# DeltaNet and a GELU layer on one core: the order of the head, from the elimination's last turn to the loads of w_out

## The chip, the cores and the metric

The kernel runs on one core of a Trainium2 chip. The metric is the device time of one execution in microseconds (us). Engines: PE (TensorE, matrix products), DVE (VectorE), ACT (ScalarE), POOL (GpSimd), SP (SyncE, which here only issues DMAs). PE's clock is throttled by the chip; the profile shows the clock that was granted, as a share of full speed.

## The reference

```
k_n = k / (norm(k) + 1e-6)
for t in range(S):                                  # B=4, H=8, S=768, D=48
    y[t]   = q[t] @ state                           # state: D x D for each batch and head
    state += beta[t] * outer(k_n[t], v[t] - k_n[t] @ state)
x   = y, reordered to 3072 x 384
h   = x @ w_in                                      # 384 x 2048
out = gelu_exact(h) @ w_out                         # 2048 x 384
```

All is float32. The weights arrive as pairs of 32-bit words, the halves of float64 values, and the kernel makes float32 of them itself.

## The kernel before, in words

**Tiles.** The 768 steps of the recurrence are cut into 12 chunks of 64; within a chunk the recurrence is solved with matrix products. A tile (c, a) is chunk c of two of the four batches: 16 heads, 8 on each half of the 128 partitions. Two chunks form a group g with four tiles, the units u of a = 0 and 1 for either chunk; `Zf`, `Nu` and `XM` hold 32 units of a group.

**The head** (from `by_hand` to `by_hand.close()`) is written out by hand: each of the five engines takes its instructions in the order of the program text. It holds

- turns of K and Q of the first chunks on PE (`transposed`, L419), each copied from PSUM by ACT (L420) into `Kt`, `Qt` or `SQ`; their Gram products (`grams`, `queries`, both through L440), copied by ACT (L451 and its neighbours);
- the elimination of group 0 (`eliminate_steps(0)`): a turn on DVE, then 30 row steps on DVE (L528 and L530), which invert the 32x32 blocks of 32 units at once in `Nu`; then three stream transposes of 128x1024, `back` 0 (L539, to `XM`) and `back` 1 and 2 (L543, to the right and the left half of `Zf`); then `clear` (L560: zeros in the lower left quarter of `Zf`, three memsets on POOL and a multiplication on ACT);
- the joins of the 32x32 blocks to 64x64 (`join`, products `psJ` at L578). Level 0 ends in DVE (L589, from PSUM to `XM`), level 1 in copies to the upper right of `Zf`;
- `against_state` for chunk 0 (V times `ng` on POOL, L722), the masking of the query products P on POOL (`masked`, L474), the scaling of V (L402), then `solve` (psU, L792), `read` (psY, L822), `turn` (x, L882) and `update` (L834) of chunk 0;
- the first decoding of w_in. A weight part goes through `begin` (exponent bits, DVE, L252 or L255), `exponents` (ACT), `mantissas` (two DVE instructions, L272 and L274) and `signed` (DVE, L281 and L282, after which the next raw part is fetched). Part n holds 256 columns of w_in for n < 8, so fc1 of f = 2n and 2n+1 needs it; parts 8 and up are pairs of rows of w_out. From part 3 on `exponents` is a pair of ACT instructions.

**The plan.** Behind the head all steps have a time in chunks, `at(first, last, steps)`; `emit` sorts them by it and writes them. DVE and POOL keep that order. PE's and ACT's instructions are placed by a scheduler, but those handed to `keep` (or `together`, `behind`) stay in the order of the program. fc1 of chunk 0 (L915, 3 matmuls into `psH`, one GELU) begins at plan time 1.0. Around 1.06 to 1.16 stand the load of chunk 3's queries, the join of chunk 1's units (`range(NA, 2 * NA)`), and V of chunk 2.

**Queues.** All loads concerned are issued by SP, one after the other, at some 0.6 us each. Before, the six transfers of w_out's first three parts (`fetch(n_in)` to `fetch(n_in + 2)`, into `w_raw`) are issued in the head ahead of V of chunk 1 (`load_v(1)`); the fourth part, which lies in the spare half of `G`, follows in the plan at 1.36.

**Two waits between engines that matter here:** `psH` and the unread products' `psI` take the PSUM tag "mlp" of two buffers, so fc1 of f + 2 waits for the GELU of f; the `sq` and `dn` tags have two buffers each as well.

Of the kernel before, what the change touches and what calls it, by code (L numbers as in the profile page):

```python
# [8 lines left out]
F32 = mybir.dt.float32  # L9
# [5 lines left out]
ALU = mybir.AluOpType  # L15
# [4 lines left out]
def kernel(  # L20
# [28 lines left out]
    nc = tc.nc  # L49
    B, H, S, D = q.shape  # L50
    DM, DF = moe_w_in.shape
    C = 64
    HB = 32
    NC = S // C
    NP = H // 2
    NA = B // 2
# [18 lines left out]
    def sq(name, *shape):  # L75
        return small[0].tile([128, *shape], F32, tag="sq", name=name)
# [189 lines left out]
        else:  # L266
            put(nc.scalar.activation, e, e, ACT.Relu, bias=lim[:, 0:1], scale=float(2 ** 23))

    def mantissas(n):
        dst, lo, hi, e = halves[n]  # L270
        bits = dst.bitcast(U32)
        nc.vector.tensor_scalar(bits, hi, 0xFFFFF, 0x100000, op0=ALU.bitwise_and,  # L272
                                op1=ALU.bitwise_or)
        nc.vector.scalar_tensor_tensor(dst, lo, 2.0 ** -32, bits, ALU.mult, ALU.add)  # L274

    def signed(n):

# [44 lines left out]
    def factors(gm, bt_, n):  # L322

        nc.vector.tensor_scalar_add(n, n, 1e-6)
        r = wk.tile([128, 2 * NA, H], F32, tag="r", name="r", bufs=1)[:, 0:n.shape[1]]
        nc.vector.reciprocal(r, n)
        nc.vector.tensor_tensor(gm, bt_, r, op=ALU.mult)
        nc.vector.tensor_tensor(gm, gm, r, op=ALU.mult)
# [144 lines left out]
    def masked(u, engine=nc.gpsimd):  # L473
        engine.tensor_tensor(u.P, u.P, mask_h, op=ALU.mult)  # L474
# [16 lines left out]
    def eliminate_steps(g):  # L491
        steps = []
        rows_on = nc.gpsimd if g > 1 else nc.vector

        def scales():
            gt = wk.tile([128, HB], F32, tag="gt", name="gt", bufs=1)
            gl = XMs[g] = wk.tile([128, NU, HB], F32, tag="XM", name="XM", bufs=1)
            nc.vector.transpose(gt, gms[g].rearrange("q t h -> q (t h)"))
            wide = gt.unsqueeze(2).to_broadcast([128, HB, HB])
            if g == 0:  # L500
                nc.gpsimd.tensor_tensor(gl, low, wide, op=ALU.mult)
            else:
                nc.gpsimd.affine_select(out=gl, in_=wide, compare_op=ALU.is_ge, fill=0.0, base=-1,
                                        pattern=[[1, HB], [-1, HB]], channel_multiplier=0)

        def flip():
            Nus[g] = wk.tile([128, HB, HB], F32, tag="Nu", name="Nu", bufs=1)
            nc.vector.transpose(Nus[g], Ds[g].rearrange("q u n -> q n u"))
            if g < 2:
                scaled_flip()  # L510

        def scaled_flip():
            rows_on.tensor_tensor(Nus[g], Nus[g], XMs[g], op=ALU.mult)

        def eliminate(j):
            nu = Nus[g]
            n = HB - 1 - j
            if j == 1 or n == 1:
                to = (slice(2, HB), slice(0, 1)) if j == 1 else (slice(HB - 1, HB), slice(0, j))
                by = (slice(2, HB), slice(1, 2)) if j == 1 else (slice(j, j + 1), slice(0, j))  # L520
                factor = nu[:, 1, 0:1] if j == 1 else nu[:, j + 1, j:j + 1]
                if g < 2:
                    nc.vector.scalar_tensor_tensor(nu[:, to[0], to[1]], nu[:, by[0], by[1]], factor,
                                                   nu[:, to[0], to[1]], ALU.mult, ALU.add)
                    return
            tmp = wk.tile([128, HB * HB // 4], F32, tag="tmp", name="tmp", bufs=1)
            tmp = tmp[:, 0:n * j].rearrange("q (i c) -> q i c", i=n)
            rows_on.tensor_tensor(tmp, nu[:, j + 1:, j:j + 1].to_broadcast([128, n, j]),  # L528
                                  nu[:, j:j + 1, 0:j].to_broadcast([128, n, j]), op=ALU.mult)
            rows_on.tensor_tensor(nu[:, j + 1:, 0:j], nu[:, j + 1:, 0:j], tmp, op=ALU.add)  # L530

        def diagonal():
            flat = Nus[g].rearrange("q i c -> q (i c)")
            rows_on.memset(flat[:, 0:HB * HB:HB + 1], 1.0)

        def back(x):
            nu = Nus[g]
            if x == 0:
                nc.vector.transpose(XMs[g].rearrange("q u c -> q c u"),  # L539
                                    nu.rearrange("q i c -> q c i"))  # L540
            elif x == 1 or g == 0:
                cols = slice(HB, C) if x == 1 else slice(0, HB)
                nc.vector.transpose(Zf[g % 2][:, :, cols].rearrange("q u i -> q i u"), nu)  # L543
            else:
                for p in range(2):
                    top = slice(p * C, p * C + HB)
                    if g > 2:
                        nc.gpsimd.tensor_copy(Zf[0][top, :, 0:HB], Zf[0][top, :, HB:C])
                    else:
                        nc.scalar.copy(Zf[0][top, :, 0:HB], Zf[0][top, :, HB:C])  # L550

        def clear(g):
                for cc in range(2):
                    for p in range(2):
                        part = Zf[g % 2][p * C + HB:(p + 1) * C,
                                         cc * NU // 2:(cc + 1) * NU // 2, 0:HB]
                        if g == cc == p == 0:
                            nc.scalar.mul(part, low[0:HB, 0:HB // 2], 0.0)
                        else:
                            nc.gpsimd.memset(part, 0.0)  # L560

        steps = [(0.3, scales), (3.0, flip)] + ([(1.2, scaled_flip)] if g > 1 else [])
        steps += [(0.7, eliminate, j) for j in range(1, HB - 1)]
        steps += [(0.1, diagonal)]
        steps += [(1.9, back, x) for x in range(3)]
        return steps + [(0.0, clear, 0)] if g == 0 else steps

    def join(g, ts, level, copy=nc.scalar.copy):

# [339 lines left out]
    def fc1(c, f):  # L909
        if c == 1 and f < EARLY:  # L910
            psH = dn("psH")[:, 0, 0:NA * 128]
        else:
            psH = ps.tile([128, NA * 128], F32, tag="mlp", name="psH")
        for m in range(NM):
            nc.tensor.matmul(psH, lhsT=w_in_sb[:, f // 2, m, f % 2 * 128:(f % 2 + 1) * 128],  # L915
                             rhs=xTs[c][:, m, :], start=(m == 0), stop=(m == NM - 1))
        gelu = G[:, :, f, :], psH.rearrange("q (a n) -> q a n", a=NA), ACT.Gelu
        if c == 0 or f < EARLY:
            keep(nc.scalar.activation, *gelu)
        else:  # L920
            nc.scalar.activation(*gelu)  # L921

    def send(u, cols=slice(0, DM), queues=None):
        queues = queues or ((nc.sync, nc.sync) if 0 < u.c < NC - 1 else (nc.scalar, nc.scalar))
# [89 lines left out]
    def keep(fn, *args, **kw):  # L1014
        i = fn(*args, **kw)  # L1015
        if free:
            tc.keep_in_program_order(i)
# [201 lines left out]
    signs(0, 2)  # L1219
    diagonals(first[3])  # L1220
    root(n0)
    scales_, flip_, *rows, back0, back1, back2, clear_ = [s_[1:] for s_ in eliminate_steps(0)]
    factors(gms[0], beta_m[:, 0:2].rearrange("q c a h -> q (c a) h"), n0)
    scales_[0]()
    flip_[0]()
    ng = wk.tile([128, NA, H], F32, tag="ng", name="ng", bufs=1)
    for u in first:
        grams([u])
    signs(2, NC)
    third = [tiles[2, a] for a in range(NA)]  # L1230
    sums_ = [(u, h) for u in third for h in range(H)]
    for u in first:
        transposed(u, (1,))
        if u.c == 1:
            for x in sums_[5 * u.a:5 * u.a + 5]:
                sum_of_squares(*x)
        queries([u])
    for a in range(NA):
        fetch_q(tiles[2, a])
# [1 line left out]
        fetch_in(Qp[2 + a][:, :, 0:D], k, tiles[3, a])  # L1241
    for n in range(2, NS):
        fetch(n)
    for n in range(n_in, n_in + 3):
        fetch(n)
    load_v(1)
    for u in third:
        transposed(u, (0,))
    for x in sums_[10:13]:
        sum_of_squares(*x)  # L1250
    grams(third)
    for u in third:
        transposed(u, (1,))
    for x in sums_[13:]:
        sum_of_squares(*x)
    fourth = [tiles[3, a] for a in range(NA)]
    for u in fourth:
        transposed(u, (0,))
    grams(fourth)
    for fn, *args in rows:  # L1260
        fn(*args)
    nc.vector.scalar_tensor_tensor(ng, gms[0][:, 0:NA], -1.0, ns[0], ALU.mult, ALU.mult)
    back0[0](*back0[1:])
    against_state(first[:NA])
    for u in first:
        masked(u)
    back1[0](*back1[1:])
    for a in range(NA):
        join(0, (a,), 0)
    back2[0](*back2[1:])  # L1270
    for a in range(NA):
        join(0, (a,), 1)
    clear_[0](*clear_[1:])
    for u in first[NA:]:
        scale_v(u)
    begin(0)
    exponents(0)
    mantissas(0)
    begin(1)
    mantissas(1)  # L1280
    solve(first[:NA])
# [27 lines left out]
    def state_at(c, *times, first=(), second=(), last=()):  # L1309

        steps = state_steps(c, first, second, last)
        if len(times) > len(steps):
# [5 lines left out]
    plan += [decode_in(), at(1.365, 1.9, decode_steps(n_in, NW)), at(1.91, 1.911, [(1.0, late)])]  # L1318
    rows1, join1 = eliminate_steps(1), join_steps(1)
    plan += [at(1.06, 1.065, [(1.0, load, 3)]),  # L1320
             [(t, (join, 0, range(NA, 2 * NA), level)) for level, t in enumerate((1.085, 1.16))],
]
    sums = [(1.0, sum_of_squares, tiles[3, a], h) for a in range(NA) for h in range(H)]
# [148 lines left out]
```

## Time and profile before

| what | us |
|---|---|
| median of 3 runs | 627.55 (626.76 to 627.88) |
| profiled execution | 626.5 |
| its span (first to last instruction) | 624.7 |
| row steps on DVE | 17.36 to 38.94 |
| the three turns on DVE, with the level 0 joins among them | 39.04 to 46.93 |
| chunk 0's solve to its update on PE | 47.91 to 56.0 |
| first fc1 on PE | 56.01 |
| six transfers of w_out issued by SP | 37.61 to 41.24 |
| first read of w_out's raw words on DVE (part 8) | 80.02 |

A page of the profile gives the busy time of each engine, the span in 40 slices with the granted clock (PEclk), the chain of work that ended last, and groups of instructions. A timeline lists start, length, engine, source line, operation, output<-inputs, shape and, in brackets, the idle time before an instruction and whose end ended it. In the weights' decoding `w_out_sb` stands for raw words of w_in, which are staged in its memory.

POOL's and SP's timelines of the stretch:
```profile
40.69 4.96 POOL L474 TENSOR_TENSOR P<-P,mask 128x512 f32<-128x512 f32 x4
47.21 2.18 POOL L560 MEMSET Zf<- 32x512 f32 x3 [1.55 <-DVE Zf L543]
51.71 2.63 POOL L402 TENSOR_TENSOR V<-V,n 128x384 f32<-128x384 f32 x2 [2.32 <-DMA V<-in_v_dram]
```
```profile
37.61 3.63 SPq L234 DMA_DIRECT2D w_raw<-in_moe_w_out_dram  x6
41.29 4.73 SPq L100 DMA_DIRECT2D V<-in_v_dram  x4
75.61 1.10 SPq L234 DMA_DIRECT2D G<-in_moe_w_out_dram  x2
```

PE's timeline from 31 to 45 us, turns (L419), Grams (L440) and joins (L578):
```profile
35.06 1.62 PE L419 MATMUL psT<-ident,Qp 128*128 128x128 f32 x8
38.21 1.15 PE L419 MATMUL psT<-ident,Qp 128*128 128x128 f32 x8 [1.53 <-ACT SQ L420]
39.98 1.98 PE L440 MATMUL psG<-Kt 48*64 48x64 f32 x64 [0.62 <-ACT Kt L420]
41.90 1.06 PE L578 MATMUL psJ<-XM,G 32*32 32x32 f32 x32
```

### The profile page before, as it was taken

The page shows a single profiled execution, that of the slowest core. Times are in us where ns is not written, and L with a number is a line of the kernel's source. Part 1 is how long each engine was busy: PE and PEld are TensorE (multiplying, and loading weights), DVE is VectorE, ACT ScalarE, POOL GpSimd, SP SyncE. Part 2 cuts the span into 40 slices and gives each one's busy share as a digit, 9 for nine tenths or more (in the row PEclk, how much of TensorE's full clock was granted, in tenths as well). Part 3 has the DMA queues.
Part 4 walks back from the last instruction along what each step waited for, and adds up shares of the span by engine and source line. Part 5 has one row for each costly group of instructions (what it writes and reads, how often), then busy time and mean ns, then how long its engine had stood idle before and what let it go on. Part 6 is the DMA issues. An engine that isn't in the chain of part 4 may idle for free.

```text
span 624.7 us, 19703 instructions
## 1 busy us (share of the span) xinstructions
PE 604.7 (97%) x8358; PEld 539.8 (86%) x8358; DVE 440.4 (70%) x811; ACT 240.5 (39%) x546; POOL 212.8 (34%) x316
## 2 busy tenths in 40 slices
PE   6789999999999999999999999999999999999997
PEld 5578786676799999998899998899998899988997
DVE  7999899988967697774859755859745947332532
ACT  3576876265443165224451134451134222044200
POOL 4045002000369821687222885222885200000000
PEclk9976999999999999999999999999999999999999
DMA  9686775101433452353123533013421001010011
GB/s 130 162 269 164 168 185 136 25 1 37 72 41 50 76 92 39 56 115 39 16 44 54 92 73 38 13 31 55 75 50 17 12 3 27 4 24 1 0 27 26
DMA packets 159576, 39.64 MB, mean 63 GB/s; under 512 B 151168, under 2 KB 154368, under 8 KB 159488
## 3 DMA queue, kind: packets, MB, share of 16 engines
q1 hardware_dynamic: 156816, 37.34, 30.7%
q10 hardware_dynamic: 2672, 1.03, 0.8%
q8 instruction: 66, 1.08, 0.7%
q14 instruction: 22, 0.18, 0.1%
HBM read 33.62 MB, written 4.72 MB: 61 GB/s over the span
## 4 chain that ended last, share of the span: by engine, by line
PE 88%; DVE 5%; ACT 3%; DMA 2%; issue 1%; SPq 0%; ACTq 0%
PE psX L966 13%; PE psY L1032 11%; PE psY L966 9%; PE psX L1032 8%; PE psZ L1032 6%; PE psV L1032 6%; PE psH L915 5%; PE psO L933 4%; PE psZ L966 4%; PE psV L966 4%; PE psG L440 3%; PE psK L732 3%; PE psY L822 2%; PE psU L792 2%; PE psQ L752 2%; PE psT L419 2%
## 5 line engine op out<-in xcount | busy, mean ns | idle before, releaser
L377 POOL TENSOR_TENSOR n<-n,half 128x16 f32<-128x16 f32 x10 | 30.8, 3079 | 178.8 <-DVE n L375 131.0
L530 POOL TENSOR_TENSOR Nu<-Nu,tmp 128x30 f32<-128x30 f32 (+14 forms) x120 | 65.3, 544 | 9.4
L528 POOL TENSOR_TENSOR tmp<-Nu 128x30 f32<-128x30 f32 (+14 forms) x120 | 62.5, 520 | 9.4
L1032 PE MATMUL psX<-xT,w_in_sb 128*128 128x256 f32 (+1 forms) x288 | 62.6, 346 | 0.0
L966 PE MATMUL psX<-w_out_sb,G 128*128 128x192 f32 x320 | 56.1, 329 | 0.0
L966 PEld LDWEIGHTS psX<-w_out_sb,G 128*128 128x128 f32 x320 | 52.2, 190 | 0.7
L1032 PEld LDWEIGHTS psX<-xT,w_in_sb 128*128 128x128 f32 x288 | 47.9, 190 | 5.4
L915 PE MATMUL psH<-xT,w_in_sb 128*128 128x256 f32 x192 | 44.6, 386 | 2.3 <-ACT G L921 1.1
L915 PEld LDWEIGHTS psH<-xT,w_in_sb 128*128 128x128 f32 x192 | 36.0, 191 | 9.6 <-ACT G L1015 2.5
L933 PE MATMUL psO<-w_out_sb,G 128*128 128x384 f32 x128 | 43.9, 490 | 0.0
L851 DVE TENSOR_TENSOR V<-psY,y 64x192 f32<-64x192 f32 (+1 forms) x60 | 21.3, 356 | 30.4 <-PE psY L834 26.4
L1060 DVE TENSOR_TENSOR psY<-psY,pu 128x512 f32<-128x512 f32 x20 | 14.0, 700 | 40.3 <-PE psY L1032 40.3
L1032 PE MATMUL psY<-xT,w_in_sb 128*128 128x256 f32 (+1 forms) x192 | 41.5, 345 | 0.0
L1015 ACT COPY xT<-psX 128x768 f32<-128x768 f32 x9 | 7.2, 800 | 79.8 <-PE psX L892 79.8
L1015 ACT COPY pu<-psZ 128x512 f32<-128x512 f32 x40 | 23.5, 587 | 37.5 <-PE psZ L1032 35.0
L933 PEld LDWEIGHTS psO<-w_out_sb,G 128*128 128x128 f32 x128 | 23.5, 190 | 14.2 <-issue 0.3
L1032 PEld LDWEIGHTS psY<-xT,w_in_sb 128*128 128x128 f32 x192 | 32.1, 191 | 3.5
L1015 ACT ACTIVATE G<-G 128x512 f32<-128x512 f32 x40 | 25.2, 631 | 21.2 <-DVE G L1068 21.0
L1068 DVE TENSOR_TENSOR G<-psY,pu 128x512 f32<-128x512 f32 x20 | 13.8, 690 | 22.2 <-PE psY L1032 21.5
L1015 ACT ACTIVATE G<-psY 128x512 f32<-128x512 f32 x20 | 11.9, 596 | 45.2 <-PE psY L1032 45.2
L966 PE MATMUL psY<-w_out_sb,G 128*128 128x192 f32 x160 | 28.1, 329 | 0.0
L966 PE MATMUL psZ<-T,pu 128*128 128x192 f32 x160 | 28.1, 329 | 0.0
(208 smaller groups left out, 1376.2 us busy)
## 6 DMA issues: line engine op xcount, KB each, us to landing
Kp<-in_k_dram SPq DMA_DIRECT2D x76, 96.0 KB, 3.2
w_out_sb<-in_moe_w_in_dram SPq DMA_DIRECT2D x24, 256.0 KB, 4.4
V<-in_v_dram SPq DMA_DIRECT2D x48, 96.0 KB, 3.1
w_raw<-in_moe_w_out_dram SPq DMA_DIRECT2D x12, 384.0 KB, 4.4
out_dram<-o_sb SPq DMA_DIRECT2D x40, 96.0 KB, 2.2
Qp<-in_k_dram SPq DMA_DIRECT2D x64, 32.0 KB, 2.2
G<-in_moe_w_out_dram SPq DMA_DIRECT2D x4, 384.0 KB, 5.1
Qp<-in_q_dram SPq DMA_DIRECT2D x96, 16.0 KB, 2.0
```

Source lines behind the costliest of these rows:

```text
L377: nc.gpsimd.tensor_tensor(flat, flat, half, op=ALU.pow)
L440: nc.tensor.matmul(psG[HALF[p], r, i * NP + j, :], lhsT=u.Kt[rows, p, j, :], rhs=(u.Qt if x else u.Kt)[rows, p, j, :], start=True, stop=True)
L528: rows_on.tensor_tensor(tmp, nu[:, j + 1:, j:j + 1].to_broadcast([128, n, j]), nu[:, j:j + 1, 0:j].to_broadcast([128, n, j]), op=ALU.mult)
L530: rows_on.tensor_tensor(nu[:, j + 1:, 0:j], nu[:, j + 1:, 0:j], tmp, op=ALU.add)
L732: nc.tensor.matmul(u.psK[HALF[p], r, j, :], lhsT=u.Kt[rows, p, j, :], rhs=SQ[rows, u.a, p ^ r, j, 0:w], start=True, stop=True)
L851: nc.vector.tensor_tensor(dst, src, pairs(u.y[at_], s), op=ALU.add)
L915: nc.tensor.matmul(psH, lhsT=w_in_sb[:, f // 2, m, f % 2 * 128:(f % 2 + 1) * 128], rhs=xTs[c][:, m, :], start=(m == 0), stop=(m == NM - 1))
L933: nc.tensor.matmul(u.psO, lhsT=G[:, u.a, f, :], rhs=w_out_sb[:, f, :], start=(f == 0), stop=(f == NF - 1))
L966: nc.tensor.matmul(ps_, lhsT=lhs[:, f, :], rhs=rhs[:, f, :], start=first and f == 0, stop=f == FH - 1, skip_group_check=not first)
L1015: i = fn(*args, **kw)
L1032: nc.tensor.matmul(ps_[:, i], lhsT=lhs[:, f // 2, f % 2 * 128:(f % 2 + 1) * 128], rhs=rhs, start=first and i == 0, stop=True, skip_group_c ...
L1060: nc.vector.tensor_tensor(L1["Y1"], L1["Y1"], L1["pu"][:, 0], op=ALU.add)
```

## The change

- **Third turn.** `back` 2 of group 0 is gone. The upper left of `Zf` is copied from its upper right by ACT (`upper_left`): units 0 to 15 behind `back` 1 and ahead of the joins, units 16 to 31 at plan time 1.05, kept in order. The lower left is cleared by two memsets on POOL ahead of the elimination. `clear` is gone.
- **Joins.** Level 1 of a = 1 is copied by DVE instead of ACT, between the two instructions of part 0's `mantissas`; `begin(0)` and `exponents(0)` come ahead of level 1.
- **Q.** Each tile of chunks 0 and 1 is turned before the query products of the tile ahead of it; K of chunk 2 likewise.
- **Unread products.** PE multiplies the identity by columns of a K tile into a PSUM tile that nobody reads. A semaphore ties the first of each set to a row step on DVE.
- **Chunk 3's Gram** comes after row step 24; its turns after row step 22. Sums of squares of chunk 2 are spread anew over ACT's list.
- **Loads.** The six w_out transfers go from the head to plan time 1.1.
- **GELUs.** All of fc1's GELUs are handed to `keep`.
- **V times `ng`** of a = 1 goes behind three of the P masks on POOL.

The diff, cut to its core:

```
-        steps += [(1.9, back, x) for x in range(3)]
-        return steps + [(0.0, clear, 0)] if g == 0 else steps
+        return steps + [(1.9, back, x) for x in range(3 if g else 2)]
+
+    def upper_left(us, put=lambda fn, *args: fn(*args)):
+        for p in range(2):
+            top = slice(p * C, p * C + HB)
+            put(nc.scalar.copy, Zf[0][top, us, 0:HB], Zf[0][top, us, HB:C])
...
-        if c == 0 or f < EARLY:
-            keep(nc.scalar.activation, *gelu)
-        else:
-            nc.scalar.activation(*gelu)
+        keep(nc.scalar.activation, *gelu)
...
     factors(gms[0], beta_m[:, 0:2].rearrange("q c a h -> q (c a) h"), n0)
+    for p in range(2):
+        nc.gpsimd.memset(Zf[0][p * C + HB:(p + 1) * C, :, 0:HB], 0.0)
     scales_[0]()
...
+    transposed(first[0], (1,))
+    for u, after in zip(first, first[1:] + [None]):
+        if after:
+            transposed(after, (1,))
+        else:
+            signs(2, NC)
+            transposed(third[0], (0,))
         queries([u])
...
-    for n in range(n_in, n_in + 3):
-        fetch(n)
     load_v(1)
-    for u in third:
-        transposed(u, (0,))
-    for x in sums_[10:13]:
+    transposed(third[1], (0,))
+    for x in sums_[:4]:
         sum_of_squares(*x)
     grams(third)
     for u in third:
         transposed(u, (1,))
-    for x in sums_[13:]:
+    for x in sums_[4:10]:
         sum_of_squares(*x)
-    for u in fourth:
-        transposed(u, (0,))
-    grams(fourth)
...
+    def unread(*cols, after=None):
+        psI = (sq("psI", 512) if after is None else
+               ps.tile([128, 512], F32, tag="mlp", name="psI"))
+        for n in cols:
+            nc.tensor.matmul(psI[:, 0:n], lhsT=ident,
+                             rhs=Kp[0].rearrange("q h d -> q (h d)")[:, 0:n], start=True, stop=True)
+            if after is not None:
+                tc.add_manual_dep(latest(mybir.EngineType.PE), after.name, ...)
+                after = None
+
+    between = {**{j: (256, 128) for j in (19, 20, 21)}, **{j: (256,) for j in (22, 23, 24, 26, 27, 28, 29, 30)}}
     for fn, *args in rows:
         fn(*args)
+        if args and args[0] in between:
+            unread(*between[args[0]], after=latest(mybir.EngineType.DVE))
+        if args and args[0] == 22:
+            for u in fourth:
+                transposed(u, (0,))
+        if args and args[0] == 24:
+            grams(fourth)
+            for x in sums_[10:]:
+                sum_of_squares(*x)
     nc.vector.scalar_tensor_tensor(ng, gms[0][:, 0:NA], -1.0, ns[0], ALU.mult, ALU.mult)
+    unread(256, 256, 256, 256, 128, after=latest(mybir.EngineType.DVE))
     back0[0](*back0[1:])
-    against_state(first[:NA])
-    for u in first:
+    against_state(first[:1])
+    for u in first[:3]:
         masked(u)
+    against_state(first[1:NA])
+    masked(first[3])
     back1[0](*back1[1:])
+    upper_left(slice(0, NA * H))
     for a in range(NA):
         join(0, (a,), 0)
-    back2[0](*back2[1:])
-    for a in range(NA):
-        join(0, (a,), 1)
-    clear_[0](*clear_[1:])
+    unread(256, 256, 128)
+    begin(0)
+    join(0, (0,), 1)
+    exponents(0)
+    mantissas(0, (0,))
+    join(0, (1,), 1, nc.vector.tensor_copy)
+    mantissas(0, (1,))
     for u in first[NA:]:
         scale_v(u)
-    begin(0)
-    exponents(0)
-    mantissas(0)
...
+             at(1.05, 1.051, [(1.0, upper_left, slice(NA * H, NU), keep)]),
+             at(1.1, 1.102, [(1.0, fetch, n_in + i) for i in range(3)]),
```

More of the change, by code (lines that the diff above doesn't have):

```diff
@@ L267, in exponents, with mantissas @@
             put(nc.scalar.activation, e, e, ACT.Relu, bias=lim[:, 0:1], scale=float(2 ** 23))
-    def mantissas(n):
+    def mantissas(n, part=(0, 1)):
         dst, lo, hi, e = halves[n]
         bits = dst.bitcast(U32)
-        nc.vector.tensor_scalar(bits, hi, 0xFFFFF, 0x100000, op0=ALU.bitwise_and,
-                                op1=ALU.bitwise_or)
-        nc.vector.scalar_tensor_tensor(dst, lo, 2.0 ** -32, bits, ALU.mult, ALU.add)
+        if 0 in part:
+            nc.vector.tensor_scalar(bits, hi, 0xFFFFF, 0x100000, op0=ALU.bitwise_and,
+                                    op1=ALU.bitwise_or)
+        if 1 in part:
+            nc.vector.scalar_tensor_tensor(dst, lo, 2.0 ** -32, bits, ALU.mult, ALU.add)
     def signed(n):
@@ L540, in back @@
                                     nu.rearrange("q i c -> q c i"))
-            elif x == 1 or g == 0:
-                cols = slice(HB, C) if x == 1 else slice(0, HB)
-                nc.vector.transpose(Zf[g % 2][:, :, cols].rearrange("q u i -> q i u"), nu)
+            elif x == 1:
+                nc.vector.transpose(Zf[g % 2][:, :, HB:C].rearrange("q u i -> q i u"), nu)
             else:
@@ L550, in back @@
                         nc.scalar.copy(Zf[0][top, :, 0:HB], Zf[0][top, :, HB:C])
[L552 to L558, printed above, removed]
-                        else:
-                            nc.gpsimd.memset(part, 0.0)
         steps = [(0.3, scales), (3.0, flip)] + ([(1.2, scaled_flip)] if g > 1 else [])
@@ L917, in fc1 @@
         gelu = G[:, :, f, :], psH.rearrange("q (a n) -> q a n", a=NA), ACT.Gelu
-        if c == 0 or f < EARLY:
-            keep(nc.scalar.activation, *gelu)
-        else:
-            nc.scalar.activation(*gelu)
+        keep(nc.scalar.activation, *gelu)
     def send(u, cols=slice(0, DM), queues=None):
@@ L1221 @@
     root(n0)
-    scales_, flip_, *rows, back0, back1, back2, clear_ = [s_[1:] for s_ in eliminate_steps(0)]
+    scales_, flip_, *rows, back0, back1 = [s_[1:] for s_ in eliminate_steps(0)]
     factors(gms[0], beta_m[:, 0:2].rearrange("q c a h -> q (c a) h"), n0)
+    for p in range(2):
+        nc.gpsimd.memset(Zf[0][p * C + HB:(p + 1) * C, :, 0:HB], 0.0)
     scales_[0]()
@@ L1228 @@
         grams([u])
-    signs(2, NC)
-    third = [tiles[2, a] for a in range(NA)]
+    third, fourth = [[tiles[c, a] for a in range(NA)] for c in (2, 3)]
     sums_ = [(u, h) for u in third for h in range(H)]
-    for u in first:
[L1233 to L1236, printed above, removed]
+    transposed(first[0], (1,))
[5 more added lines that the diff above has]
+            transposed(third[0], (0,))
         queries([u])
@@ L1253, with latest @@
         transposed(u, (1,))
-    for x in sums_[13:]:
+    for x in sums_[4:10]:
         sum_of_squares(*x)
-    fourth = [tiles[3, a] for a in range(NA)]
-    for u in fourth:
-        transposed(u, (0,))
-    grams(fourth)
+    def latest(engine):
+        return next(i for i in reversed(nc.cur_bb.bb.instructions) if i.engine == engine)
+    def unread(*cols, after=None):
[5 more added lines that the diff above has]
+            if after is not None:
+                tc.add_manual_dep(latest(mybir.EngineType.PE), after.name,
+                                  mybir.DependencyInfo(mybir.DependencyClass.Sync,
+                                                       mybir.DependencyReason.DATA),
+                                  reason="time")
+                after = None
@@ L1262 @@
     nc.vector.scalar_tensor_tensor(ng, gms[0][:, 0:NA], -1.0, ns[0], ALU.mult, ALU.mult)
+    unread(256, 256, 256, 256, 128, after=latest(mybir.EngineType.DVE))
     back0[0](*back0[1:])
-    against_state(first[:NA])
-    for u in first:
+    against_state(first[:1])
+    for u in first[:3]:
         masked(u)
+    against_state(first[1:NA])
+    masked(first[3])
     back1[0](*back1[1:])
+    upper_left(slice(0, NA * H))
     for a in range(NA):
         join(0, (a,), 0)
-    back2[0](*back2[1:])
```

## The prediction

> **What bounds the kernel now.** I read the totals and slices first, then the chain that ended last, then the timelines of DVE, ACT and PE from 38 to 70 us, where every edit lies.
>
> The page's totals and three of its slice rows (40 slices of 15.6 us):
> ```profile
> span 624.7 us, 19703 instructions
> PE 604.7 (97%) x8358; PEld 539.8 (86%) x8358; DVE 440.4 (70%) x811; ACT 240.5 (39%) x546; POOL 212.8 (34%) x316
> ...
> PE   6789999999999999999999999999999999999997
> ...
> DVE  7999899988967697774859755859745947332532
> ...
> PEclk9976999999999999999999999999999999999999
> ```
> PE (TensorE) is at 9 tenths or more from the fourth slice on, and PEclk, the granted clock, is below full in the first four alone. So a change in the head is worth what it moves PE's first dense work, and no more. In windows, PE is busy 5.87 of 6 us from 70 to 76 and all of 76 to 104. In the chain that ended last DVE stands from 44.3 to 66 (the elimination's end, then the decoding of w_in), PE and ACT from 66 to 76, PE to 88, DVE to 103, then PE to the end.
>
> DVE's timeline (start, length, instruction, in brackets its idle time before and who ended it):
> ```profile
> 43.02 0.86 DVE L589 TENSOR_TENSOR XM<-psJ,gm 32x256 f32<-32x256 f32 x2
> 44.27 0.86 DVE L589 TENSOR_TENSOR XM<-psJ,gm 32x256 f32<-32x256 f32 x2 [0.39 <-PE psJ L578]
> 45.16 1.93 DVE L543 STREAM_TRANSPOSE Zf<-Nu 128x1024 f32<-128x1024 f32 x1
> 46.93 0.55 DVE L255 TENSOR_SCALAR w_e<-w_out_sb 128x768 uint32<-128x768 uint32 x1
> 47.39 0.97 DVE L272 TENSOR_SCALAR w_in_sb<-w_out_sb 128x768 uint32<-128x768 uint32 x1
> ...
> 49.74 0.55 DVE L272 TENSOR_SCALAR w_in_sb<-w_out_sb 128x768 uint32<-128x768 uint32 x1
> ```
> DVE hardly rests: whatever leaves its list brings w_in forward. ACT's and PE's timelines where decoding, GELUs and joins meet:
> ```profile
> 61.53 2.12 ACT L1015 ACTIVATE w_e<-w_e,lim 128x768 f32<-128x768 int32 x2 [1.93 <-DVE w_e L252]
> 63.52 0.35 ACT L1015 ACTIVATE G<-psH 128x256 f32<-128x256 f32 x1
> 63.77 2.11 ACT L1015 ACTIVATE w_e<-w_e,lim 128x768 f32<-128x768 int32 x2
> ...
> 67.37 1.17 ACT L593 COPY Zf<-psJ 32x512 f32<-32x512 f32 x2 [1.00 <-PE psJ L578]
> ```
> ```profile
> 61.53 1.56 PE L915 MATMUL psH<-xT,w_in_sb 128*128 128x256 f32 x6
> 63.93 1.56 PE L915 MATMUL psH<-xT,w_in_sb 128*128 128x256 f32 x6 [0.83 <-ACT G L1015]
> ...
> 66.14 1.19 PE L578 MATMUL psJ<-Zf,XM 32*32 32x32 f32 x62 [0.48 <-DVE XM L589]
> ```
> The chain here is: DVE writes the raw exponents of part 3, ACT maps them for 2.12 us, only then comes the GELU of f2, which frees the PSUM tile that fc1 of f4 waits for (0.83 us). After 67.27 PE waits for next to nothing.
>
> **The change part by part.** First DVE, up to part 0's L255.
>
> *Third turn gone.* L589 ends at 45.13, L255 starts at 46.93: −1.80. *psJ in time.* The 0.39 before the second L589 goes if psJ is ready: −0.39. *Two copies from PSUM added* (join level 1 of a=1, 32x256): the nearest row is L589, same shape and source, 0.86 for two: +0.86. *Clearing of Zf.* POOL's memsets (47.21, 2.18 us) lay over L272, 0.97 against 0.55 for the same line at 49.74; they move to the start: −0.42. There, as two ops of 32x1024, they lie around 7 to 10 us, ahead of the scaling of `low` at 14.15; by the same row they can lengthen a DVE op there by 0 to 0.5, and I take 0, since DVE waits in that stretch anyway.
>
> *New neighbours.* POOL masks P from 40.69 to 45.65 in four ops of 1.24. L255 of part 0 now starts while the fourth runs. Nearest row: L255 at 53.69 beside POOL's scaling of V (51.71 to 54.34) took 1.07 against 0.55. Between 0 (L255 comes after 45.65) and the length of a whole mask op, 1.24; I take +0.75, between that and the row's 0.51. The two stretched ops beside the scaling of V (1.47 against 0.96, 1.07 against 0.55) stay.
>
> [...]
>
> *Unread products.* Identity times Kp, 256 columns each, after rows 19 to 30, after `ng` and between the joins. Nearest row: fc1 (L915) has the same width; in the chain x12 take 2.86 and x24 take 5.38 us, 0.21 for one record, and a product is two: 0.43 at the full clock, double at half. After `ng` (38.9) stand 4 of 256 and one of 128: 2.0 us. PE's order before psJ is now: turns of chunk 3, two products, Gram, five products, these, psJ. Chunk 3's K is issued up to 32.6 and lands between 35.0 and 37.3. Landing at 35.5: turns to 36.1, Gram to 37.7, five products to 39.9, `ng` products to 41.9, psJ half a microsecond per half: ready before L589 can start at 43.02. Landing at 37.3: everything 1.6 to 2.2 later, psJ at 44 to 44.6, DVE waits 1.0 to 1.6. These same microseconds clear the collision with P. So from 0 to +1.6 in place of, not beside, the +0.75.
>
> Sum for DVE: −1.80 −0.39 +0.86 −0.42 +0.75 = **−1.0**, with bounds −1.75 (no collision, psJ in time) and +0.24 (−1.80 +0.86 −0.42 +1.6: psJ 1.6 late), more if the products also run slow.
>
> The clock, which the products concern, in the windows view (PE, PEld, DVE, ACT, POOL busy, then granted clock):
> ```profile
> 39.50:39.70 0.20, 0.00 (x0) 0.00 (x0) 0.20 (x1) 0.20 (x1) 0.20 (x1) 0.77 0.83 287
> 39.70:40.00 0.30, 0.02 (x3) 0.02 (x3) 0.30 (x1) 0.30 (x2) 0.30 (x2) 0.50 0.75 287
> 56.00:57.00 1.00, 1.00 (x7) 0.87 (x4) 1.00 (x2) 0.40 (x1) 1.00 (x1) 0.66 0.06 16
> 57.00:57.50 0.50, 0.50 (x4) 0.43 (x3) 0.47 (x2) 0.00 (x0) 0.50 (x1) 1.00 0.06 25
> ```
> PE ran at half clock from 39.6 to about 56.7, through both joins, psU, psY and the turns of x (dense from 47.91 to 56.01). With products in place of the pause 36.7 to 38.2 I expect it fast. That halves some 8 us of PE, but f0 to f3 then wait for w_in's parts, which DVE sets: worth 0 to 0.4 by itself.
>
> *Upper-left copies on ACT.* Two in place of the third turn's first half, 32x512 from SBUF to SBUF; nearest row, the diag copies of the same shape, 1.24 for two. The first pair runs from about 43, while DVE does L589, and psJ level 1 doesn't read it; psU does, which PE reaches later: 0. The second pair is issued behind part 3's exponents and ahead of f2's GELU: **+1.24** on the chain ACT to f4. Thus f4 starts at 63.93 − 1.0 + 1.24 = +0.24 later. *What takes it up:* PE's 0.48 in front of psJ level 1 falls, since its L589 comes 1.0 earlier on DVE. It leaves f5 and all behind it at +0.24 − 0.48 = −0.24; the first 0.7 us of fc1, which ran at half clock from 56.01, are worth 0.3 more: about **−0.5**. In short, the end moves by DVE's shift + 0.46. From there PE is dense, so −0.5 is carried to the end.
>
> *Q turned one tile ahead.* PE waited 0.67 us four times (21.63 to 30.19) for ACT's copies of Q; they go, but the third Gram waits for K and DVE's rows (17.36 to 38.94) wait for none of it: 0. If it failed, the row steps would still set 38.94. *Squares of chunk 2* (20, 0.14 to 0.2 each) move inside ACT's idle time: 0.
>
> *w_out later.* Six transfers of 384 KB leave SP's queue at 37.61 (3.63 us of issuing) and go to 75.6, in front of chunk 4's K (76.76). V of chunk 1 is issued 3.7 earlier and POOL's 2.32 us wait for it goes; what follows at 76.76 comes some 3.6 later, needed from about 100 on. The first of w_out lands, at 6 to 7 us apiece beside each other, at about 79 to 80; DVE's first read of it is at 80.02. A wait of 0 to 1.0: I take 0, since DVE waits 0.53 and 0.35 for PE near 87 and catches up there. *GELUs in order*: their order in ACT's list is unchanged: 0.
>
> Total: −0.5 against the profiled 626.5 (span 624.7 and 1.8 around it), so 626.0. That execution is 1.05 under the median of 627.55; on the median I get **627.0**.
>
> **The rivals.**
> *Better cover.* K lands by 35.5 and L255 misses the P op, or loses 0.4 at most: DVE −1.75, f4 at 63.93 − 1.75 + 1.24 = −0.51, with psJ's 0.48 and the faster f0 make −1.3; if f4's wait on the GELU (0.83) shrinks too, because f2 itself is ready sooner, up to −2.1: **625.8** in the middle. For it: most transfers of these 10 us land 2.4 to 3.0 us after their issue, which is 35 to 35.6. Against: L255 at 44 to 45 falls in front of 45.65 as worked out.
>
> *Products hold up psJ (slower).* The change doesn't do what it says if the clock falls at 39.6 all the same. Then the `ng` products take 3.9 instead of 2.0. With K at 35.5 they end at 43.8, the first psJ half (1.06 at that clock) at 44.8, L589 is 1.8 late and DVE at +0.24; each 0.1 us that K is later costs 0.2. With K at 36.0 DVE is at about +1.2, f4 at +2.4, less 0.48 and with no gain of clock: +2.0 at the end, **629.5**; with K at 37.3 it is up to +5. It eats the whole gain from 0.9 us of psJ's delay on (−1.36 + 0.9 + 0.46), and is slower by 0.2% from 1.9 on. For it: PE has a fixed order and the products stand ahead of psJ; against: the two turns on DVE leave 4 us between the rows' end, 38.94, and 43.02, and the products themselves fill the pause after which the clock fell.
>
> [...]
>
> *w_out comes late.* Landing 2.5 us after DVE's read at 80.02, beyond the slack of 0.9: −0.5 + 1.6, **628.6**.
>
> **How the numbers follow.** Forecast 0.42, of it 0.06 below 626.3; better cover 0.32; held-up psJ 0.15; pause moved 0.07; w_out late 0.04. A measurement of this kernel tells 0.2%, or 1.25 us, from no change. Faster 0.32 + 0.06 = 0.38; slower 0.15 + 0.07 + 0.02 = 0.24, and 0.02 more for an unhidden w_out: 0.26; same 0.36. Range: 624.8 (better cover at its far end, 625.4, with the two ops beside V's scaling also gone, 0.5) to 630.0 (the pause at 3.4 less f4's 0.83 is +2.6).
>
> **What would show it.** Right: no third turn, L255 of part 0 at about 45.9; granted clock 1.00 from 36 to 57; first f4 near 64.2; f5 near 66.8; PE dense behind it. Wrong: psJ level 0 after 43; L255 at 47 or later; clock 0.50 anywhere past 57; part 8's L255 with DVE idle ahead of it; f4's wait on GELU over 1.5.

## The result, and the profile after

| | before | changed |
|---|---|---|
| median, us | 627.62 (4 runs) | 633.02 (4 runs, 631.65 to 633.75) |
| profiled execution, us | 626.5 | 633.3 |
| span, us | 624.7 | 631.6 |

The ratio is 1.0086, 95% interval 1.0066 to 1.0106: 5.4 us slower, where 0.5 faster was forecast and 630.0 was the end of the range. The changed kernel's page (totals, and the granted clock over 40 slices of 15.8 us):

```profile
span 631.6 us, 19804 instructions
PE 609.0 (96%) x8402; PEld 542.3 (86%) x8402; DVE 438.6 (69%) x812; ACT 242.0 (38%) x547; POOL 211.2 (33%) x315
...
PEclk9879899999999999999999999999999999999999
```
PE has 44 records more (22 unread products, two records each) and 4.3 us more busy time; its clock is below full in the fifth slice too.

A good first reading sets the same instruction of both traces beside each other and lists how late the changed kernel is. On DVE:

| before, at | late by | what happened just ahead |
|---|---|---|
| 19.3 | 0.7 | PE waited 0.81 instead of 0.25 near 13, the diagonal blocks came later |
| 44.3 | 2.7 | L589 (now L585) waited for psJ |
| 57.2 | 0.6 | the removed turn and the vanished collisions gave it back |
| 77.2 | 2.6 | f4 waited, then ran at half clock |
| 83.4 | 3.7 | DVE waited for w_raw |
| 91 to 316 | 3.5 | nothing: PE is dense in both |
| 327.2 | 5.5 | PE stood still for 1.90 us |
| 420.0 to the end | 6.8 to 6.9 | PE stood still for 0.96 us |

DVE behind the second turn, in the changed kernel's timeline (start, length, instruction, idle time before):
```profile
46.12 1.75 DVE L585 TENSOR_TENSOR XM<-psJ,gm 32x256 f32<-32x256 f32 x4 [2.33 <-PE psJ L574]
47.90 0.65 DVE L255 TENSOR_SCALAR w_e<-w_out_sb 128x768 uint32<-128x768 uint32 x1
...
49.10 0.86 DVE L589 COPY Zf<-psJ 32x256 f32<-32x256 f32 x2
```
The wait for psJ, 0.39 before, is 2.33, and the two added copies take 0.86 as forecast. PE's timeline says why, and shows the later pause ahead of f4:
```profile
33.23 4.90 PE L1258 MATMUL psI<-Kp,ident 128*128 128x256 f32 x14
...
41.07 4.37 PE L1258 MATMUL psI<-Kp,ident 128*128 128x256 f32 x20
45.38 1.20 PE L574 MATMUL psJ<-XM,G 32*32 32x32 f32 x64
...
65.77 2.92 PE L911 MATMUL psH<-xT,w_in_sb 128*128 128x256 f32 x6 [2.79 <-ACT G L1008]
```
The first 14 records (six of them with 128 columns only) take 0.35 each and the 20 ahead of psJ 0.22. But for turns and a Gram (37.93 to 41.07, two products among them) PE does nothing else from 33.2 on, and psJ stands behind all of it. ACT's timeline around the pause:
```profile
62.09 2.13 ACT L1008 ACTIVATE w_e<-w_e,lim 128x768 f32<-128x768 int32 x2 [2.73 <-DVE w_e L252]
64.09 1.21 ACT L1008 COPY Zf<-Zf 32x512 f32<-32x512 f32 x2
65.33 0.38 ACT L1008 ACTIVATE G<-psH 128x256 f32<-128x256 f32 x1
```
The second pair of copies stands, 1.21 us long, in front of f2's GELU, which frees f4's tile. The windows view (PE, PEld, DVE, ACT, POOL busy, then the granted clock) of the three stretches:
```profile
33.00:37.40 4.40, 4.40 (x16) 3.86 (x15) 3.99 (x13) 2.41 (x14) 0.00 (x0) 0.50 0.90 208
62.90:65.70 2.80, 0.07 (x1) 0.00 (x0) 2.51 (x4) 2.73 (x5) 0.00 (x0) 0.99 0.81 238
65.80:69.20 3.40, 3.40 (x31) 2.39 (x32) 3.30 (x6) 2.64 (x4) 0.00 (x0) 0.52 0.95 278
```
The early products ran at half clock; the pause of 2.8 us is followed by 3.4 us at half clock, in which fc1's six records take 2.92 instead of 1.56. Last, on DVE and on PE, two waits that the head's order doesn't show:
```profile
85.68 0.56 DVE L255 TENSOR_SCALAR w_e<-w_raw 128x768 uint32<-128x768 uint32 x1 [1.00 <-DMA w_raw<-in_moe_w_out_dram]
```
```profile
326.23 0.97 PE L959 MATMUL psZ<-T,pu 128*128 128x192 f32 x5 [1.90 <-issue]
```
"issue" means that PE waited for nothing that the profile shows.

### The profile page after: what moved, and what is told of

The parts are those of the page before. It is cut to its first block, busy times and chain, and to the rows that moved or that the text cites. A ratio compares the mean times of both kernels' runs of the same rounds, so it can differ in the third digit from the quotient of the medians.

```text
span 631.6 us, 19804 instructions
## 1 busy us (share of the span) xinstructions
PE 609.0 (96%) x8402; PEld 542.3 (86%) x8402; DVE 438.6 (69%) x812; ACT 242.0 (38%) x547; POOL 211.2 (33%) x315
## 3 DMA queue, kind: packets, MB, share of 16 engines
q8 instruction: 66, 1.08, 0.7%
## 4 chain that ended last, share of the span: by engine, by line
PE 85%; DVE 4%; DMA 4%; SPq 3%; issue 2%; ACT 2%; ACTq 0%; DVEq 0%
PE psX L959 13%; PE psY L1025 11%; PE psY L959 8%; PE psX L1025 8%; PE psV L1025 6%; PE psZ L1025 6%; PE psO L926 4%; PE psZ L959 4%; PE psV L959 4%; PE psH L911 3%; PE psK L728 3%; PE psY L818 2%; SPq L100 2%; DMA Kp<-in_k_dram 2%; PE psG L442 2%
## 5 line engine op out<-in xcount | busy, mean ns | idle before, releaser
L911 PE MATMUL psH<-xT,w_in_sb 128*128 128x256 f32 x192 | 46.1, 393 | 5.3 <-ACT G L1008 4.6
L911 PEld LDWEIGHTS psH<-xT,w_in_sb 128*128 128x128 f32 x192 | 36.4, 194 | 13.4 <-ACT G L1008 7.0
```

## The experiments

**Theory:** the loss is a sum of parts that have little to do with one another: late w_out, the second pair with the clock that falls behind it, products ahead of psJ, and PE's stalls of 1.90 and 0.96 us. **Rival:** one part makes the others late, so that undoing it brings most of the loss back. The kernel before, run on the same chip beside each group of them, had medians of 627.0 to 627.3. Runs of one kernel with products spread by 2 to 5 us, so differences under about 1 us between such medians are not told apart.

**w_out back.**
```
+    for n in range(n_in, n_in + 3):
+        fetch(n)
     load_v(1)
...
-             at(1.1, 1.102, [(1.0, fetch, n_in + i) for i in range(3)]),
```


> Changed kernel with the six w_out transfers issued in the head again, ahead of V of chunk 1. Theory (the loss is a sum of parts, and late w_out is one of them: DVE waited 1.00 us for w_raw at 84.7 and its lag grew from 2.6 to 3.7 there): 1.0 us faster than the changed kernel's 633.0, so 632.0, with no DVE wait on w_raw. Rival (those waits are covered by DVE's later waits for PE): 633.0 within 0.3. The two stalls of PE without a visible releaser, 1.90 us at 324 and 0.96 at 418, stay if they belong to PE's own instruction stream, which is the same here, and go if they were caused by the loads.

632.63 us (631.08 to 633.06): the wait for w_raw is gone, but the time falls by 0.4 only, which is within the spread. In the trace the pause ahead of f4 is still 2.79 and DVE waits up to 3.3 us for ACT behind it. Undoing one of several parts measures only what the next one leaves. PE's stalls are there (1.66 and 0.68): the w_out loads didn't make them.

**Pair early.**
```
-    upper_left(slice(0, NA * H))
+    upper_left(slice(0, NU))
...
-             at(1.05, 1.051, [(1.0, upper_left, slice(NA * H, NU), keep)]),
```


> Changed kernel with both pairs of upper-left copies in the head, behind the second turn, none in front of f2's GELU. Theory (the second pair, 1.21 us on ACT, lengthens PE's wait ahead of f4 from 0.83 to 2.79, and this pause drops the clock to half from 65.8 to 69.2): f4 waits 1.2 to 1.6, no half clock near 66, f5 2.0 to 2.6 earlier, 630.7. Rival (the pause is set by DVE's part 3 alone and the clock falls anyway): f4 at most 0.6 earlier, 632.4 or more.

632.30 us (630.35 to 633.93). f4's wait is 1.52, and f5 follows at 0.23 us a record, without half clock, as the theory had it, 1.6 earlier (2.0 to 2.6 expected); but DVE now meets w_raw earlier and waits 2.1 for it, and the time moves by 0.7, within the spread, where 2.3 was expected. In the profiled execution, the slowest of the four, the lead over the changed kernel was down to 0.6 at PE's first stall, and there more was lost:
```profile
325.64 4.34 PE L959 MATMUL psZ<-T,pu 128*128 128x192 f32 x16 [1.90 <-issue]
```
The granted clock is 0.50 from 325.5 to 328.8, so these 16 records take 4.34 instead of 2.76, and the kernel ends 0.6 later than the changed one. In this trace half clock thus stands behind the stall; behind the changed kernel's, as long, the granted clock is 1.00 from 324 to 331.

**No products, and no late products.** All of `unread`'s calls out, or those behind `ng` and between the joins.

> Changed kernel without any unread product; all of the reference is still computed. Theory (products at half clock filled PE from 33.2 to 45.4 and held psJ back; DVE waited 2.33 for it): psJ level 0 before 43.0, no wait of DVE there, part 0's L255 2.3 us earlier at about 45.6, f4 earlier by as much: 630.9. Rival (the products keep the clock up; without them psJ, psU and psY run at half clock and eat the gain): clock 0.50 from 40 to 57 and 632.5 or more.

> Changed kernel with the products of the row steps, but without the 4.5 behind ng and the 2.5 between the joins. Theory: the 2.0 us of products right ahead of psJ are the part that delays it; DVE's wait falls from 2.33 to about 0.4, L255 2 us earlier, with the clock still full from 38 on: 631.1, no slower than the kernel without any product. Rival (the delay comes from the products at rows 19 to 24, which ran at half clock): DVE's wait stays above 1.5 and the time near 632.5.

628.07 us (10 runs) without any: the largest step, −5.0, more than the 2.1 expected. psJ is in time, L255 at 44.90. The clock is 0.50 around the joins (64 records of psJ take 1.92 and 1.95, where they took 1.20 in the changed kernel), as the rival has it, and the gain is there all the same. PE's two stalls are gone. Without the late ones 629.2 (631.1 expected): DVE's wait is gone too (L585 at 43.02), so the theory's half about psJ holds, but one stall of 0.78 stays near 415, and f4 waits 2.26 with half clock behind it. Why did taking out products in the head end stalls at 324 and 418?

**PE's code.** The page counts what the engines' code moves:
```profile
q8 instruction: 66, 1.08, 0.7%
```
66 transfers, 1.08 MB: 16 KB each. PE has 8402 matmul records with a weight load each, 16,804 instructions. If this queue is PE's, an instruction has about 64 bytes, and a block 256 of them: the author's estimate from these numbers. The run psQ, psU, psG near 317 (before) has 192 records and lasts 3.2 us, thus a block lasts 2.1 us there, while the products behind it (L966) take 0.18 us a record, a block 23 us. A transfer in this queue took 0.9 us (before, 317 to 325: one, 0.7% of 16 engines' 8 us) to 1.5 (changed, 320 to 327: one, 1.3% of 7 us). By this estimate a shift of 88 instructions, a third of a block, moves the places where blocks end. Two kernels test it, with products of 4 columns in PE's first idle time:
```
+    psI = sq("psI", 512)
+    for _ in range(22):          # 42 in the changed kernel
+        nc.tensor.matmul(psI[:, 0:4], lhsT=ident, rhs=ident[:, 0:4], start=True, stop=True)
     load_v(0)
```


> Kernel before with 22 products of 4 columns (identity times identity, read by nobody) in the idle time ahead of PE's first turn; these make as many PE instructions as the changed kernel's 22 unread products do. Theory (PE's code comes in blocks of 16 KB, 256 instructions; 88 more instructions shift where a block ends, and a block that ends inside the short runs psQ, psU, psG is used up faster than the next one lands): the stalls of 1.9 us near 320 and 0.7 to 1.0 near 413 appear in this kernel too, 629.6. Rival (the stalls come from the changed head's times or loads): no such stall, 627.0 within 0.4.

> Changed kernel with 42 products of 4 columns in the idle time ahead of PE's first turn: with its own 22 these are 64 products, 256 instructions, one whole block of code, so that its blocks end where those of the kernel before do. Theory: both stalls go, 633.0 less 2.7, 630.3, and what is left above 627 is the head's own loss of about 3.5. Rival: the stalls stay, 633.0 or a little more.

636.65 and 645.43 us: as times both missed, since the small products aren't small (44 records took 9.55 us, 0.217 each, far over the idle 2.8) and made the whole head late. The traces still answer. In the kernel before, with 88 instructions more, the stalls appear:
```profile
330.69 2.06 PE L966 MATMUL psZ<-T,pu 128*128 128x192 f32 x11 [0.60 <-issue]
...
423.00 0.70 PE L440 MATMUL psG<-Kt 48*64 48x64 f32 x33 [0.71 <-issue]
```
In the changed kernel, shifted by a whole block, they are gone, and its lag behind the changed kernel falls there by 1.70 and 1.29:
```profile
338.51 1.16 PE L442 MATMUL psG<-Kt 48*64 48x64 f32 x64
339.60 2.71 PE L959 MATMUL psZ<-T,pu 128*128 128x192 f32 x15
```
The page of this kernel, with 256 instructions more than the kernel before, has 67 transfers in that queue where all others have 66. The kernel before isn't free of such stalls either; it has one at another place:
```profile
244.98 0.38 PE L834 MATMUL psY<-V,Kp 64*48 64x48 f32 x11 [0.47 <-issue]
```
All sixteen traces have that one, 0.20 to 1.02 long. Counted in PE's matmul records it comes behind 3766 to 3772 of them in fifteen traces, and behind 3894, some 128 more, in the kernel shifted by a block. The other two come behind 4910 to 4915 and 6181 to 6185 in all five traces with 8402 records, though up to 9 us apart in time; the distances, 1144 and some 1271 records, are 9 and 10 times 127.1, about a block. A cause in the head's times or in the loads wouldn't keep to a count. Thus the count of PE instructions ahead decides whether PE stalls at these two places; it is shown both ways. That PE waits there for its code is the author's reading of the counts and was not shown: in the changed kernel a transfer of that queue starts at 323.1 and takes 1.5, another at 416.8 and takes 1.3, so both end well before the stalls do, at 326.23 and 419.53. How long it stalls (0.60 to 1.90 at the first place in five traces with the same count) is not settled; K's loads are issued in the same microseconds (four of 96 KB from 320 to 327 in the changed kernel).

**The other two corners, and the corners between.** Products, pair and w_out can each be as in the changed kernel or undone; with the three of the first group and the changed kernel itself, four more runs complete the eight. The outcome stands between the two readings. Without the products alone 4.95 us come back, as the rival has it, but 1.1 are left, and what a part costs depends on the others: they don't simply add.

> Changed kernel without any unread product and with both pairs of upper-left copies in the head. Theory (without products psJ is in time; the second pair on ACT costs its 1.21 us ahead of f2's GELU): 1.0 to 1.5 faster than the kernel without products alone (628.1), so 626.8, no wait of DVE on ACT above 1 us between 60 and 76; w_raw may be waited for by up to 1 us. Rival (ACT's pair is covered there, since f4 didn't wait in that run): 628.0.

> The same with the six w_out transfers in the head again. Theory (an earlier DVE meets w_out's landing at 83 to 85, as in the run with the pair early, which waited 2.1): 0.5 to 1.0 faster than the run before it, 626.0. Rival (transfers in the head delay w_in's parts and V of chunk 1): 627 or more.

> Changed kernel with both pairs of copies in the head and the w_out transfers in the head, the unread products left as they are. Only they then separate it from the run without products, pair early, w_out in the head (626.4). Theory (the products cost the wait of DVE for psJ, about 2.3, and 2.7 by where PE's blocks of code end): 631.0, with both stalls near 324 and 418. Rival (late w_out and the pair were most of the loss): 628.5 or less.

> No products, w_out in the head, but the second pair of copies ahead of f2's GELU as in the changed kernel. Against the run with the pair early (626.4) it gives the pair's price alone. Theory: f4 waits about 1.2 longer, 627.4. Rival (covered): 626.4.

| medians, us | no products | products |
|---|---|---|
| pair early, w_out in the head | 626.43 | 629.76 |
| pair at 1.05, w_out in the head | 627.35 | 632.63 |
| pair early, w_out late | 628.65 | 632.30 |
| pair at 1.05, w_out late (the changed kernel's) | 628.07 | 633.02 |

Products cost 3.3 alone and 3.7 to 5.3 beside others. The pair costs 0.9 alone, with products 2.9, where the pause ahead of f4 is 2.79 and fc1's six records behind it take 1.90, the next six 2.93, instead of 1.56 (w_out back). With w_out late it is +0.7 beside products and −0.6 without, neither clear of the spread. Late w_out costs 2.2 alone and 2.5 with products, but only 0.4 to 0.7 where the pair has made DVE late already: a later reader waits less. My expectation for the run with the pair early and no products (626.8) missed for this reason: DVE was earlier and waited 3.3 us for w_raw, and the granted clock was 0.50 for 3.4 us behind it. That for the pair alone (627.4) hit the time by luck: f4 doesn't wait in its trace, since fc1 ahead of it is held up by half clock until 60 (15 records in 4.58 from 57.54 on), and where the 0.9 arises is not shown (the two profiled executions are 0.3 apart). That for the products alone (631.0) was 1.2 too high; its trace, the fastest of six runs, has both stalls (0.96 and 0.72) and a wait for psJ of 1.1. There PE is at full clock from 33.8 on, and the first 14 records take 2.56 instead of 4.90:
```profile
34.07 2.56 PE L1260 MATMUL psI<-Kp,ident 128*128 128x256 f32 x14
```

**Single parts on the kernel before.** The turn alone, with `upper_left` for all units behind `back` 1 and the early memsets; and w_out alone.

> Kernel before with one part alone: no third turn, both pairs of copies on ACT behind the second turn, the lower left cleared early; no other edit, the same PE instructions. Theory (DVE is the bound there and loses 1.80 of work and 0.42 of collision, gains 0.75 of another): part 0's L255 at about 45.2, 626.0, the whole gain of the best variant or more. Rival (that variant's gain came from Q turned ahead and the Gram's place): 627.0.

> Kernel before with one part alone: the six w_out transfers issued at plan time 1.1 instead of in the head. Theory (w_raw lands at 83 to 85, DVE reads at 80.0 and has 0.9 of slack near 87): DVE waits 2 to 3 us for w_raw at 80 to 84, 628.9. Rival (loads covered, V of chunk 1 earlier): 627.2.

The turn alone: 625.48 us (626.0 expected), ratio 0.9971 (0.9960 to 0.9983), 1.7 faster. w_out late alone: 630.01 us (628.9 expected), ratio 1.0046 (1.0032 to 1.0059), 2.8 slower, against the 1.6 that the prediction's last rival gave it. DVE in the two:
```profile
45.39 0.68 DVE L255 TENSOR_SCALAR w_e<-w_out_sb 128x768 uint32<-128x768 uint32 x1
```
```profile
82.97 0.56 DVE L255 TENSOR_SCALAR w_e<-w_raw 128x768 uint32<-128x768 uint32 x1 [1.86 <-DMA w_raw<-in_moe_w_out_dram]
```
L255 of part 0 stood at 46.93, the one of w_raw at 80.02. In the second trace DVE is 0.9 late at the first L589 already, long ahead of w_raw, and why is not shown; so not all of the 2.8 need be the loads'. The table has 2.2 for the same move in the changed order.

**The last 0.95.** The best corner (626.43) is still 0.95 above the turn alone. Suspects: the two copies on DVE, or Q, the Gram and the sums in their new places. In one run the copies go to DVE in the fast kernel, in the other back to ACT in the best corner:
```
-    join(0, (1,), 1, nc.vector.tensor_copy)
+    join(0, (1,), 1)
```


> The run with the third turn replaced alone (625.5), with the level 1 copies of a = 1 from PSUM moved from ACT to DVE, between part 0's exponent bits and its mantissas, as the changed kernel has them. Theory (DVE is the bound in this stretch, and two copies take 0.86 of it): 626.3. Rival (psU and the decoding gain by it as much as DVE loses): 625.5.

> The best variant of the changed kernel (no products, pair early, w_out in the head: 626.4) with those two copies on ACT again. Theory: 625.6, as fast as the kernel before with only the turn replaced; Q turned ahead, the Gram's place and the rest are then worth nothing either way. Rival (one of those costs the 0.95 between 626.4 and 625.5): 626.4.

627.03 and 625.41 us: the copies cost 1.55 (in that run DVE also waits 0.47 for psJ ahead of them) and 1.02, and with them back on ACT the changed order is as fast as the turn alone (625.48). Q turned ahead, chunk 3's Gram later, the moved sums and the kept GELUs together are worth nothing measurable. This last kernel is 1.85 us faster than the kernel before, ratio 0.9963 (0.9950 to 0.9976); from the turn alone it can't be told apart.

## Why the prediction was wrong, step by step

- **Third turn, −1.80:** right; alone, collision and all, it gave 1.7 at the end. *Two copies from PSUM, +0.86:* right in kind, 1.0 to 1.55 at the end. *New collision, +0.75:* right: 1.32 and 1.35 against 0.55 for L255 where psJ was in time; in the changed kernel L255 came later and took 0.65, the other branch that the prediction gave. *Early memsets, 0:* right, DVE was 0.12 late at 13.4. (The 0.81 of PE near 13 varied from nothing to 1.3 over the runs, and 1.29 stands in a kernel without them.)
- **psJ in time, −0.39 and 0 to +1.6:** the step that failed first, by the path that it gave PE. It let chunk 3's turns start when K lands, at 35.5, and gave no time to the seven products of rows 19 to 22, which stand ahead of them in PE's order. These took 4.90 us, from 33.23 on, and the turns began at 37.93. Nearly half of that was the clock, 0.50 until past 37.4; with the pair early and w_out in the head, at full clock, they took 2.56. From the turns to psJ the working has 6.4 us, 35.5 to 41.9, and 7.45 passed: eight turns are put at 0.6 where they took 1.1, and two products and the Gram at 1.6 where they took 2.05. So psJ came at 45.38, and DVE waited 2.33; even at full clock it came at 43.69, and DVE waited 1.09. Neither of the causes that the prediction named for late products (K landing at 37.3, a clock that falls at 39.6) was it.
- **Second pair, +1.24 on ACT:** the row was right (1.21), the balance wasn't. DVE stood at +0.6 and not at −1.0, and with that the prediction's own sum, 63.93 + 0.6 + 1.24, gives the 65.77 at which f4 started. The pause of 2.79 was followed by 3.4 us of half clock, for which the sum has no term. The case of a moved pause had a chance of 0.07. No run shows the 3.4 from which the range's upper end is worked out: behind the pause of 2.79 fc1's six records took 2.92 instead of 1.56, 1.4 us more.
- **w_out late, 0:** wrong, and at 2.2 to 2.8 alone dear, though undoing it in the changed kernel gave back only 0.4. The prediction let the first transfers land at 79 to 80; of the pair that was issued at 75.6 before, one landed at 79.5 and the other at 81.8. In the changed kernel six of them, issued from 76.91 to 80.01 behind the loads that the plan puts ahead, landed one after another from 81 to 87.6; DVE's first read, late itself at 82.66, found its pair there, the second waited 1.00. The row of 6 to 7 us, added to an issue at 75.6 and later, would have said so.
- **The clock in the head, 0 to 0.4:** right that it matters little, as the fastest kernels have 0.50 around the joins, but the expected 1.00 from 36 on came at 38.4 only. PEclk misled here: digits 9, 9, 7, 6 put only the third and fourth slice below nine tenths, not the first four, and the Gram of 64 records at 33.15 in the kernel before took 1.99, as long as the one at 39.98 under a granted 0.50, though the windows show 1.00 there. Early in the span PE's speed is read from the length of its records.
- **PE's code:** no term at all. The 44 more records were counted as time, not as a shift of the code; in the profiled run the two stalls were 2.9 of the 6.9 us.
- **The chances:** held-up psJ, moved pause and late w_out were taken as cases that exclude each other, each near 629 or 630. They came together, and two of them feed one another. A range from single cases can't hold that; their sum on the forecast, 627.0 + 2.5 + 2.6 + 1.6, would have been 633.7. That this is near the measured 633.0 is luck, since it holds nothing for PE's stalls.

## What to carry to other kernels

Mishaps that sit at different places of one path add up, so a range needs the case in which several of them happen. Work that is added to fill an engine stands in that engine's order: ask what waits behind it when the clock is at its lowest, and what its instructions do to the code that follows. Price a move of loads from the issue time of the last transfer and the landing time of that many side by side, against the first read; and when several parts are suspected, measure the corners, since undoing one alone (0.4 for w_out) may hide what it costs alone (2.8).

## What the runs showed of the hardware that was not expected

- PE stood still for 0.6 to 1.9 us with no releaser in the profile, behind the same 4910 to 4915 and 6181 to 6185 matmul records in the five traces with 8402 of them, some 290 us and more after the edit. The kernel before had neither stall, with 88 more PE instructions it had both; the changed kernel had both, and neither with 168 more. That PE waits for its code there is the author's reading of these counts. Kernels whose PE instruction count was that of the kernel before had no such stall near 320 and 415, only the one near 245 that all have.
- A stall or pause of PE of 1.9 to 2.8 us was followed by 3.4 us at half clock in some traces (changed kernel at 65.7, pair early at 325.5), and not in others (changed kernel behind its stall of 1.90 at 324.3).
- A product of 4 columns is not cheaper than its weight load: 0.217 us a record at the start, where the weight loads fill 9.46 of the 9.55 us, and nearly as much as the turns of 128 columns right behind (eight in 1.95, 0.24 each).
- Spread: six runs of one kernel with products (pair early, w_out in the head) lay between 628.4 and 633.4 us, six of the turn alone between 625.3 and 626.2. In the traces of kernels with products PE's stalls differ in length, and one was followed by half clock (pair early); whether that makes the first spread is not shown.
